# A fused attention and expert kernel on one core: batch 2's loads, the first moves, W0's split and expert 0's first blocks change their places

## The chip, the cores and the metric

The kernel runs on one core of a Trainium2 chip. The metric is the device time of one execution in microseconds (us); less is better. The core has TensorE (PE in the profile; its weight loads are PEld), VectorE (DVE), ScalarE (ACT), GpSimd (POOL) and SyncE (SP). SP computes nothing: it issues nearly all DMA transfers, in the order of the program, and an issue whose data or buffer isn't ready holds every later issue of SP.

## What is computed

Decayed causal attention over 8 batches, 8 heads, 576 positions and a head size of 64, and then a layer of 8 experts with a sticky choice of the expert, on the 8 x 576 tokens of 512 numbers that attention leaves:

```python
decay = cum[:, :, :, None] - cum[:, :, None, :]          # cum: running sum of log(clip(f))
scores = where(causal, -1e9, scale * q @ k.T + decay)
attn = exp(scores - max); attn = attn / (sum + 1e-9)
x = (attn @ v), heads side by side                        # 8 x 576 x 512
# per token: e = argmax of x @ w_gate, or the token before's e if sigmoid(x @ w_local) >= 0.5
p = softmax(x @ w_gate)
out = p[e] * (relu(x @ w1[e]) @ w2[e])                    # w1: 8 x 512 x 1024, w2: 8 x 1024 x 512
```

## The kernel before

**Numbers.** Values that meet on TensorE are split into a float16 high part and a low part (two or three products in place of one). For q, k, v of a batch POOL makes the parts, four to eight instructions each; for weights it is POOL (`early_weights`, four pieces for a block of 128 x 1024) or ACT and DVE (`weights`).

**Attention.** One batch after another. A batch has 25 units (`compute`): the chunks of 128 queries of two heads, and at the end five units for the last 64 queries. A unit runs sc (scores, PE, line L895: a product of `Ak`, `Aq` and one of `KB`, `QB`), mx (DVE L906), ex (ACT L926), tr (PE L941), hi (ACT L946), lo (DVE L950) and av (PE L920). L1001 runs once in a batch, when the last units begin. The order of all instructions of each engine is written out when the program is built: `issue` keeps a clock for each engine and takes the stage that can start first, with weights `W` and ranks `RANK`. So every engine has one fixed list, and an instruction that waits holds all behind it.

**Loads and turns.** q and k of a batch come from memory into `ldq` and `ldk` (L164, L171: 2 transfers of 512 KB and 2 of 64 KB each), POOL splits them into `t16q` and `t16k`, PE turns them (L477, groups of eight tiles: `tq`, `eq`) into `Aq`, `Ak`, and SP copies the high parts into `QB`, `KB` (L397, L394, L401: within SBUF). For batch 0 the turning is done by DMA (L381 to L389). The moves of batch 0 and 1 stand in three hand-written lists, `ORD0`, `ORDA`, `ORDB`; `DUE` gives the times, on the builder's clock, at which the turning of heads 2 and 3, the splits of v and the lists A and B are placed. The move `2` of `ORDB` issues the loads of batch 2, in the middle of batch 0. From then on loads go through the list `bulk`, which `ship` empties, one entry for each unit, when an entry's unit number and condition are met. Copies are kept back (`hold_back`) until the builder's clock has reached the end of what they copy.

**Side work.** `chain` holds the routing of earlier batches (gate products L843, `route`), which `issue` puts between the stages. Routing's `marks` (L1511 to L1525) are DVE's largest. After batch 6's tokens are routed, `early_tok` gathers the first 3 x 128 tokens of experts 0 and 1 (POOL L1677, three buffers) and turns them by DMA (L1679).

**Between attention and experts.** In batch 7 `early_weights` loads (L1642) and splits the first four blocks of expert 0's weights `W0` (all of its w1) on POOL, in portions that `pump` gives out unit by unit; the loads go through three buffers, so that the fourth waits until block 0 is split. Behind attention `flow` orders several streams by their own clocks: `products` (expert 0's and 1's first products, L2087: 8 blocks of 12 matmuls, 128 x 384 each, for either expert), `hidden` (L2122 on ACT, L2124 on DVE), `outputs` (L2102: 3 tiles of 24 matmuls for either expert), the last batch's routing, the rest of the weights (`blocks`, L1851 on ACT and L1855 on DVE) and the gathers of the other tokens (`fetch`, L2178, L2184). The streams have priorities, and PE's list is made of them in the order of the clocks. Then `fixed(0)` (L1709, L1695) and the other experts run, PE nearly without a break.

## Time and profile before

| | |
|---|---|
| time, median of 3 runs | 824.3 us (821.01 to 827.14) |
| the profiled execution's own time | 821.98 us |
| its span, first to last instruction | 820.2 us |
| PE busy | 764.8 us, 93% of the span |
| mean granted clock of TensorE | 0.986 of 2.4 GHz |
| DVE, ACT, POOL busy | 522.6, 437.7 and 398.6 us |
| moved by DMA | 121.99 MB |

All sums are made against 821.98 us. Times of single instructions are us from the start of the span. A timeline row has the start, the duration, the engine, the line, the operation with what it writes and reads, how many, and in brackets the engine's idle time before it and what ended that. PE counts as busy while a matmul is in flight, so a busy PE needn't be at its peak.

### The profile page before, as it was taken

To read this page: it belongs to the slowest core of one execution; us is meant where nothing else is said; L and a number is where in the kernel's file an instruction comes from. 1 tells how busy PE (TensorE), PEld (TensorE's weight loads), DVE (VectorE), ACT (ScalarE), POOL (GpSimd) and SP (SyncE) were. 2 spreads that over 40 slices of the span, in tenths; PEclk is the share of its full clock that TensorE was granted. 3 is DMA by queue.
4 is the path that set the end of the run, shared out by engine and by line. 5 is a ranking of instruction groups with operands and counts; after the bars stand their busy time and mean duration, and the time that the engine had idled before them with its cause. 6 is when DMAs were issued, how large, how long until landed. Compare 5 with 4: busy or idle time off the path is not lost. (4 is left out here: it accounts for less than half of the span.)

```text
span 820.2 us, 21911 instructions
## 1 busy us (share of the span) xinstructions
PE 764.8 (93%) x8918; PEld 544.9 (66%) x8918; DVE 522.6 (64%) x1147; ACT 437.7 (53%) x816; POOL 398.6 (49%) x465
## 2 busy tenths in 40 slices
PE   5798999989999999988879999999999999999996
PEld 3586888877887788866544565675665857667453
DVE  7685879899888999898689813253272744526020
ACT  5595879777887888766633224343241423325121
POOL 9699929388884959572635213131302313031102
PEclk9898999999999999998999999999999999999999
DMA  7969938687594949177693922766282754817101
GB/s 175 192 155 186 216 82 161 156 159 192 106 226 97 186 106 184 26 162 162 122 299 136 266 65 89 187 180 173 101 228 94 192 162 136 218 68 200 53 1 49
DMA packets 195336, 121.99 MB, mean 149 GB/s; under 512 B 135099, under 2 KB 171197, under 8 KB 195212
## 3 DMA queue, kind: packets, MB, share of 16 engines
q1 hardware_dynamic: 189169, 101.42, 54.3%
q0 software_dynamic: 6064, 19.14, 7.2%
q8 instruction: 71, 1.16, 0.6%
q14 instruction: 32, 0.26, 0.1%
HBM read 72.15 MB, written 19.36 MB: 112 GB/s over the span
## 5 line engine op out<-in xcount | busy, mean ns | idle before, releaser
L926 ACT ACTIVATE P<-st,nm 128x512 f32<-128x512 f32 (+3 forms) x288 | 152.9, 587 | 28.4 <-DVE nm L906 25.3
L1696 DVE SCALAR_TENSOR_TENSOR hl<-z,hh 128x608 f16<-128x608 f32 (+5 forms) x64 | 43.0, 673 | 168.1 <-ACT hh L1695 167.2
L1709 PE MATMUL z<-xT,wh 128*128 128x304 f16 (+5 forms) x832 | 147.2, 293 | 1.3 <-DVE hl L1696 1.3
L946 ACT CAST ph<-pt 128x512 f16<-128x512 f32 (+1 forms) x200 | 116.1, 584 | 51.4 <-PE pt L941 46.0
L906 DVE TENSOR_REDUCE nm<-st 128x1 f32<-128x512 f32 (+4 forms) x264 | 134.3, 542 | 14.3 <-PE st L902 11.5
L941 PE MATMUL pt<-ident,P 128*128 128x128 f32 x784 | 122.7, 280 | 7.7 <-DVE pl L950 5.9
L950 DVE TENSOR_TENSOR pl<-pt,ph 128x512 f16<-128x512 f32 x168 | 111.3, 668 | 13.8 <-ACT ph L946 12.2
L1701 POOL DMA_INDIRECT out_dram<-o,ranki x23 | 23.5, 1021 | 168.4 <-ACT o L1700 152.4
L1736 PE MATMUL y<-uh,hl 128*128 128x512 f16 (+2 forms) x440 | 101.0, 309 | 0.3 <-issue 0.3
L941 PEld LDWEIGHTS pt<-ident,P 128*128 128x128 f32 x784 | 84.9, 142 | 24.5 <-issue 6.5
L1736 PE MATMUL y<-uh,hh 128*128 128x512 f16 (+2 forms) x440 | 101.1, 311 | 0.0
L1736 PE MATMUL y<-ul,hh 128*128 128x512 f16 (+2 forms) x440 | 100.8, 309 | 0.0
L1709 PEld LDWEIGHTS <-wh 128*128 128x128 f16 x832 | 81.3, 98 | 29.1 <-issue 1.7
L1709 PE MATMUL z<-xT,wl 128*128 128x304 f16 (+5 forms) x416 | 95.8, 293 | 0.0
L920 PE MATMUL xp<-VH,pl 128*128 128x65 f16 (+1 forms) x960 | 91.5, 195 | 3.5 <-DVE pl L950 3.5
L920 PE MATMUL xp<-VH,ph 128*128 128x65 f16 (+1 forms) x960 | 93.3, 197 | 0.0
L920 PE MATMUL xp<-VL,ph 128*128 128x65 f16 (+1 forms) x960 | 92.2, 196 | 0.0
L1736 PEld LDWEIGHTS <-hh 128*128 128x128 f16 (+2 forms) x880 | 56.7, 100 | 52.7 <-issue 5.2
L920 PEld LDWEIGHTS <-ph 128*128 128x128 f16 (+1 forms) x1920 | 84.6, 103 | 6.8 <-issue 2.8
L1695 ACT ACTIVATE hh<-z 128x608 f16<-128x608 f32 (+5 forms) x64 | 37.3, 583 | 95.5 <-PE z L1709 91.4
L895 PE MATMUL st<-KB,QB 70*128 70x256 f16 (+4 forms) x448 | 78.3, 283 | 8.7 <-DMA KB<-Ak 8.7
L895 PE MATMUL st<-Ak,Aq 128*128 128x256 f16 (+4 forms) x448 | 78.4, 285 | 3.8 <-ACT P L926 2.7
(383 smaller groups left out, 1427.8 us busy)
## 6 DMA issues: line engine op xcount, KB each, us to landing
stg<-in_moe_w_dram SPq DMA_DIRECT2D x64, 512.0 KB
xs<-xr SPq DMA_DIRECT2D x16, 512.0 KB
ldq<-in_q_dram SPq DMA_DIRECT2D x14, 512.0 KB
ldk<-in_k_dram SPq DMA_DIRECT2D x14, 512.0 KB
ldv<-in_v_dram SPq DMA_DIRECT2D x28, 256.0 KB
QB<-Aq SPq DMA_DIRECT2D x15, 256.0 KB
KB<-Ak SPq DMA_DIRECT2D x15, 256.0 KB
ldv<-in_v_dram SPq DMA_DIRECT2D x20, 64.0 KB
```

Of the source, the lines that this page charges most:

```text
L895: nc.tensor.matmul(st[p0:p0 + m, co:co + n], lhsT=queries(lq, kk, h, c), rhs=rhs, start=(ps == 0 and first and co == col), stop=(ps == 1), ...
L906: nc.vector.tensor_reduce(dst, src, axis=AX.X, op=ALU.max, negate=True)
L920: nc.tensor.matmul(xo, lhsT=a[:, c0:c0 + m], rhs=w[:, vi, :], start=False, stop=(i == n - 1 and jj == 2), skip_group_check=True)
L926: nc.scalar.activation(P[:, c0:c1].rearrange("p (k x r) -> p k r x", r=2, x=64), st[:, c0:c1].rearrange("p (k r x) -> p k r x", r=2, x=64) ...
L941: nc.tensor.matmul(U["pt"][:, i * 128:(i + 1) * 128], lhsT=P[:, i * 128:(i + 1) * 128], rhs=ident, is_transpose=True, start=(i == 0), stop ...
L946: nc.scalar.copy(U["ph"][:, :cols], U["pt"][:, :cols])
L950: nc.vector.tensor_tensor(U["pl"][:, :cols], U["pt"][:, :cols], U["ph"][:, :cols], ALU.subtract)
L1695: nc.scalar.activation(hv, z[:, 0:nh, 0:wd], AF.Relu)
L1696: nc.vector.scalar_tensor_tensor(lv, z[:, 0:nh, 0:wd], 0.0, hv, ALU.max, ALU.subtract)
L1701: nc.gpsimd.indirect_dma_start(out=outf, out_offset=bass.IndirectOffsetOnAxis(ap=scat(t), axis=0), in_=o, in_offset=None, bounds_check=NT ...
L1709: nc.tensor.matmul(z[:, a, 0:wd], lhsT=w[:, d, fc * 128:(fc + 1) * 128], rhs=xT[:, x, a * wd:(a + 1) * wd], start=(i == 0), stop=(i == len ...
L1736: nc.tensor.matmul(y[m * r:m * r + m, 0:w], lhsT=a[:, fc, c0:c0 + m], rhs=u[:, fc, w * r:w * r + w], start=(i == 0), stop=(i == len(prods) ...
```

## The change

Batch 2's loads are not issued in `ORDB` any more. The move `2` puts three entries for q and three for k on `bulk`, with the condition that all of batch 1's main groups are turned; what is left of them at the start of batch 1 is issued there, before `prep(2)` adds its own. In `ORD0` the move `sv` (v's heads 6 and 7, POOL) goes to the front, `k:l` (SP) in front of `q:t4`, `q:p` (POOL) behind `sp`, and `q:M` (SP) in front of `k:t`; `ORDA` and `ORDB` swap three pairs. Three times of `DUE` change. `PB` makes POOL's portions of W0 end at unit 14 in place of 23. `z_lines` puts the first `NZ` = 3 of expert 0's 8 product blocks into batch 7's list from unit 12 on: four stages of three matmuls, one ACT and one DVE stage for each block, in a bank of `psS`, not before `early_tok` plus 10.5 us on the builder's clock and not before POOL's queue is given out; `products` and `hidden` begin with block 3. In `flow` PE's routing steps are planned as if what they wait for came 1.5 us later (`LATE`). `SX` and `SQ` leave the value 0 that was there. Core of the diff:

```diff
--- before.py
+++ after.py
@@ -40,9 +40,9 @@
 
 
 
-ORD0 = moves_of("q:l :k2 q:t4 k:l q:p k:t4 :sp q0:m :sv k:p q:c k:c q1:m q:t k:t :lm q:M k:m :at 0:R 1:R :lv")
-ORDA = moves_of("q0:P k:M 0:V 1:V k:ag")
-ORDB = moves_of("q:ag q:G0 2:V q1:P k0:P k1:P q:e k:e 3:V q:G1 k:G0 :vl :Vl q:2 k:G1 :iv v0:P k:2")
+ORD0 = moves_of("q:l :k2 :sv k:l q:t4 k:t4 :sp q:p q0:m k:p q:c k:c q1:m q:t q:M k:t :lm k:m :at 0:R 1:R :lv")
+ORDA = moves_of("k:M q0:P 0:V 1:V k:ag")
+ORDB = moves_of("q:ag q:G0 2:V q1:P k0:P k1:P k:e q:e 3:V q:G1 k:G0 :vl :Vl k:G1 q:2 :iv v0:P k:2")
 
 GM, GW = 8, 500
 
@@ -60,12 +60,19 @@
 HB = (1, 1)
 ST = 4
 XP = 20
+PB = 14
+NZ = 3
+LATE = 1500
+SX = {}
+SQ = [0]
+Z0 = 12
+ZT = 10500
 XG = 6
 NP0 = 4
 SB = 3
 
 T0 = 9700.0
-DUE = (("k2", 11000), ("q2", 12500), ("k3", 14500), ("q3", 15500), ("v", 18000), ("v4", 20500), ("a", 26000), ("b", 29000))
+DUE = (("k2", 11000), ("q2", 12500), ("k3", 14500), ("q3", 15000), ("v", 18000), ("v4", 19500), ("a", 26000), ("b", 30000))
 
 NB = (4, 5, 4)
 NOV = 31
@@ -664,10 +671,17 @@
         elif a == "sv":
             split_v(6, 8)
         elif a == "2":
-            new_load(2, b)
-            for C in range(2):
-                load_main(2, b, C, 0, H)
-            load_last(2, b)
+            c = lambda: all((1, x, j) in turned for x in 'qk' for j in range(4))
+
+            def some(C):
+                if C == 0:
+                    new_load(2, b)
+                if C < 2:
+                    load_main(2, b, C, 0, H)
+                else:
+                    load_last(2, b)
+
+            bulk.extend([(0, c, lambda C=C: some(C)) for C in range(3)])
         elif a == "R":
             same_rows(int(b))
         elif a == "t4":
@@ -1152,7 +1166,7 @@
 
     WAIT = {("PE", "PE"): 0, ("PE", "ACT"): 197, ("PE", "DVE"): 196, ("ACT", "PE"): 227, ("ACT", "ACT"): 150,
             ("ACT", "DVE"): 141, ("DVE", "PE"): 200, ("DVE", "ACT"): 128, ("DVE", "DVE"): 127}
-    STAGES = ("sc", "mx", "mn", "ex", "tr", "hi", "lo", "sub", "lo2", "av", "n1", "n2", "tq", "eq")
+    STAGES = ("sc", "mx", "mn", "ex", "tr", "hi", "lo", "sub", "lo2", "av", "n1", "n2", "tq", "eq", "z0", "z1", "z2", "z3", "zh", "zl")
     RANK = {st: 0.0 for st in STAGES + ("side",)}
     RANK["side"] = -20
     RANK.update({'sc': 24.3, 'mx': 16.8, 'mn': -67.5, 'ex': 93.3, 'tr': -65.0, 'hi': 26.5, 'lo': -10.3, 'sub': 17.2, 'lo2': 31.3, 'av': 16.7, 'n1': 33.1,
@@ -1160,6 +1174,8 @@
     W = {st: 0 for st in RANK}
     W.update({'sc': -210, 'mx': -60, 'mn': -710, 'ex': -30, 'tr': -180, 'hi': -210, 'lo': -140, 'sub': -410, 'lo2': -360, 'av': -130, 'n1': -200,
               'n2': -170, 'tq': -210, 'eq': -50})
+    RANK.update({'z0': 90, 'z1': 90, 'z2': 90, 'z3': 90, 'zh': 90, 'zl': 90})
+    W.update({'z0': 300, 'z1': 300, 'z2': 300, 'z3': 300, 'zh': 0, 'zl': 0})
     clock = {"PE": T0, "ACT": T0, "DVE": T0, "POOL": T0}
     due = deque()
     pools = {}
@@ -1176,7 +1192,11 @@
         after = []
         if st == "tq":
             after.append((u["ready"], "POOL"))
-        elif prev is not None or st != "sc":
+        elif st == "z0":
+            if queue or "ready" not in EX:
+                return None
+            after += [(EX["ready"], "POOL"), (clock["POOL"], "POOL")]
+        elif prev is not None or st not in ("sc", "z0"):
             dep = (n, prev) if prev is not None else (n - 1, "ex")
             if dep not in ends:
                 return None
@@ -1226,7 +1246,7 @@
 
         if t is None:
             return 0
-        return SW[0] if cost is POOL or t <= clock[eng] + SW[2] else SW[1]
+        return SW[0] if cost is POOL or t <= clock[eng] + SQ[0] else SW[1]
 
     def side_issue(t, eng, cost):
         fn = chain[0]
@@ -1777,13 +1797,57 @@
         EX["p"] = probs(invp[:, :, 0:NE], NE, "x")
 
     def early_tok():
+        EX["ready"] = max(clock["DVE"], clock["POOL"]) + ZT
         for e in range(2):
             xT = EX["xT", e] = ep.tile([128, 8, 128 * EARLY], F16, name=f"xT{e}")
             tokens(ep, xT, lambda i: EX["g"][:, CAP * e + i:CAP * e + i + 1], EARLY, (B - 2) * S)
 
+    HID = {}
+    EM = 128 * EARLY
+
+    def z_part(fc, z, i0, i1):
+        wh, wl = W0[0:2]
+        prods = [(w, d, x) for d in range(ND) for w, x in ((wh, d), (wh, ND + d), (wl, d))]
+        for i in range(i0, i1):
+            w, d, x = prods[i]
+            nc.tensor.matmul(z, lhsT=w[:, d, fc * 128:(fc + 1) * 128], rhs=EX["xT", 0][:, x], start=(i == 0), stop=(i == len(prods) - 1))
+
+    def z_unit(fc):
+        Z = {}
+
+        def mm(k):
+            if k == 0:
+                Z["z"] = psS.tile([128, 512], F32, name="st")[:, 0:EM]
+            z_part(fc, Z["z"], 3 * k, 3 * k + 3)
+
+        def hh():
+            if fc == 0:
+                HID["hh", 0] = ep.tile([128, NF, EM], F16, name="hh")
+                HID["hl", 0] = ep.tile([128, NF, EM], F16, name="hl")
+            nc.scalar.activation(HID["hh", 0][:, fc], Z["z"], AF.Relu)
+
+        def hl():
+            nc.vector.scalar_tensor_tensor(HID["hl", 0][:, fc], Z["z"], 0.0, HID["hh", 0][:, fc], ALU.max, ALU.subtract)
+
+        u = {f"z{k}": ("PE", 490, lambda k=k: mm(k), {"psS": 1} if k == 0 else {}, {}) for k in range(4)}
+        u["zh"] = "ACT", 400, hh, {}, {}
+        u["zl"] = "DVE", 480, hl, {}, {"psS": 1}
+        return u
+
+    def z_lines():
+        for fc in range(NZ):
+            n, prev, u = serial[0] + 100 + fc, None, z_unit(fc)
+            for st in ("z0", "z1", "z2", "z3", "zh", "zl"):
+                line[st].append((n, u, prev))
+                prev = st
+
     gated = set()
     for b in range(B):
+        SQ[0] = SX.get(b, 0)
         units = compute(b, Tq[b])
+        if b == 1:
+            while bulk and bulk[0][0] == 0:
+                bulk.popleft()[2]()
         if 0 < b < B - 1:
             queue.extend(prep(b + 1))
         for i, u in enumerate(units):
@@ -1793,9 +1857,11 @@
                 init_gate()
             if not due:
                 if b < B - 1 or i < XP:
-                    pump((23 if b == B - 1 else 25) - i)
+                    pump((PB if b == B - 1 else 25) - i)
                 ship(i if i < 24 else 99)
                 add_turns(i)
+            if b == B - 1 and i == Z0:
+                z_lines()
             step(u)
             if b == B - 1:
                 if i == 5:
@@ -2039,7 +2105,7 @@
                     after.append(h[3])
                 if op.get("opens"):
                     after.append(lock["free"])
-                t = max([clk.get(eng, t0), op.get("from", 0) + t0] + [e + (0 if src == eng else 200 if src != "SP" else 0) for e, src in after])
+                t = max([clk.get(eng, t0), op.get("from", 0) + t0] + [e + (LATE if eng == "PE" and op.get("seq", True) and h[0] < -4999 else 0) + (0 if src == eng else 200 if src != "SP" else 0) for e, src in after])
                 able.append((t, h[0], h))
             first = min(able, key=lambda x: x[0])
             t, _, h = min((x for x in able if x[2][2]["eng"] == first[2][2]["eng"] and x[0] <= first[0] + 300), key=lambda x: x[1])
@@ -2065,8 +2131,6 @@
         return dict(eng=eng, cost=cost, fn=fn, needs=needs, gives=gives, **kw)
 
     XP0 = EX["xT", 0], EX["xT", 1]
-    HID = {}
-
     def products():
 
         m = 128 * EARLY
@@ -2074,8 +2138,7 @@
             W = W0 if e == 0 else EX["W"]
             wh, wl, uh, ul = W
             xT = XP0[e]
-            hh = hl = None
-            for fc in range(NF):
+            for fc in range(NZ if e == 0 else 0, NF):
                 n = NF * e + fc
                 prods = [(w, d, x) for d in range(ND) for w, x in ((wh, d), (wh, ND + d), (wl, d))]
                 for c in range(0, len(prods), 2):
@@ -2087,7 +2150,7 @@
                             nc.tensor.matmul(HID["z", n][:, 0, 0:m], lhsT=w[:, d, fc * 128:(fc + 1) * 128], rhs=xT[:, x, 0:m],
                                              start=(i == 0), stop=(i == len(prods) - 1))
                     needs = [("hl", n - 2)] if c == 0 and n > 1 else []
-                    if fc == 0:
+                    if fc == (NZ if e == 0 else 0):
                         needs += [("w", e, prods[c + 1][1])]
                     yield op_("PE", 330, fn, needs, [("z", n)] if c + 2 == len(prods) else [])
             for t in range(EARLY):
@@ -2112,11 +2175,11 @@
     def hidden(part):
 
         m = 128 * EARLY
-        for n in range(2 * NF):
+        for n in range(NZ, 2 * NF):
             def fn(n=n):
                 e, fc = divmod(n, NF)
                 if part == 0:
-                    if fc == 0:
+                    if ("hh", e) not in HID:
                         HID["hh", e] = ep.tile([128, NF, m], F16, name="hh")
                         HID["hl", e] = ep.tile([128, NF, m], F16, name="hl")
                     nc.scalar.activation(HID["hh", e][:, fc], HID["z", n][:, 0, 0:m], AF.Relu)
@@ -2258,7 +2321,7 @@
         yield from blocks(first, NP, ST + 3 - NP, 1)
 
     FW = static_weights(W0, 0, NP0, ahead=SB, ha=HB)
-    ready = op_(None, 0, nop, gives=[("w", 0, d) for d in range(ND)])
+    ready = op_(None, 0, nop, gives=[("w", 0, d) for d in range(ND)] + [("hl", n) for n in range(NZ)])
     e0 = CAP + EARLY
     flow([(-9000, iter([ready])), (-3000, products()), (-6000, hidden(0)), (-6000, hidden(1)), (-4400, outputs(0)), (-4400, outputs(1)),
           (-5600, routing()), (-5000, third_pair()), (-5500, blocks(FW, NP0, SB, 0)), (-300, second()), (-4400, second_rest()),
```

## Rows read from the trace of the kernel before

**Rows 1.** Page, part 1: busy time, share of the span, instructions

```profile
PE 764.8 (93%) x8918; PEld 544.9 (66%) x8918; DVE 522.6 (64%) x1147; ACT 437.7 (53%) x816; POOL 398.6 (49%) x465
```

**Rows 2.** PE's waits, whole span: us in total, times, longest

```profile
PE st L895 <- DMA KB<-Ak: 8.7, 3, 5.0
...
PE psG L1582 <- ACT kg L1420: 2.3, 1, 2.3
PE psG L1445 <- DVE crow L1441: 2.0, 1, 2.0
```

**Rows 3.** Windows, two early stops: length, busy us (instructions), PEclk, DMA share, GB/s

```profile
30.50:36.00 5.50, 0.50 (x8) 0.27 (x5) 1.65 (x3) 1.42 (x4) 1.28 (x4) 0.95 1.13 241
...
70.50:74.00 3.50, 0.10 (x1) 0.20 (x2) 0.65 (x2) 0.19 (x1) 3.40 (x4) 0.85 1.19 171
74.00:80.00 6.00, 6.00 (x76) 4.50 (x76) 2.90 (x6) 2.44 (x5) 5.39 (x8) 0.52 0.87 142
```

**Rows 4.** SP's timeline, batch 2's first load and batch 1's copy

```profile
56.19 1.21 SPq L164 DMA_DIRECT2D ldq<-in_q_dram  x2
...
66.77 2.78 SPq L394 DMA_DIRECT2D KB<-Ak  x2
```

**Rows 5.** PE's timeline, batch 1's first scores

```profile
73.90 0.59 PE L895 MATMUL st<-KB,QB 70*128 70x512 f16 x1 [3.40 <-DMA KB<-Ak]
```

**Rows 6.** Line L1001, batches 0, 1, 2: min/median/max ns, first to last start

```profile
L1001 PE MATMUL st<-mB,mA x4: 193/193/203, 55.7 to 55.8; 128*128 128x64 f16 x4
...
L1001 PE MATMUL st<-mB,mA x4: 193/193/203, 106.5 to 106.6; 128*128 128x64 f16 x4
...
L1001 PE MATMUL st<-mB,mA x4: 193/193/202, 149.8 to 149.9; 128*128 128x64 f16 x4
```

**Rows 7.** Windows of batch 1 and its end; columns as in rows 3

```profile
80.00:100.00 20.00, 19.85 (x297) 17.02 (x295) 18.18 (x42) 17.42 (x36) 19.20 (x23) 1.00 1.00 192
...
105.00:120.00 15.00, 14.75 (x308) 12.36 (x307) 12.14 (x30) 11.86 (x26) 3.33 (x3) 1.00 0.21 44
```

**Rows 8.** Windows, attention's last 15 us and the transition

```profile
393.00:408.00 15.00, 11.79 (x257) 9.28 (x257) 10.09 (x24) 10.10 (x21) 11.42 (x10) 1.00 0.60 111
408.00:440.00 32.00, 25.11 (x199) 13.80 (x193) 26.48 (x70) 10.05 (x18) 15.95 (x15) 1.00 0.87 266
```

**Rows 9.** POOL's timeline in batch 7: first gather, block 3's split

```profile
382.18 1.24 POOL L1677 DMA_INDIRECT xg<-xs,xg  x1 [10.36 <-DVE xs L1617]
...
408.42 1.04 POOL L1651 TENSOR_SCALAR stg<-stg 128x1024 f32<-128x1024 f32 x1
```

**Rows 10.** DVE's timeline, the same operation with POOL busy and idle

```profile
367.62 1.50 DVE L1525 TENSOR_TENSOR LO<-i,lo 128x640 f16<-128x640 f16 x1
...
441.31 1.55 DVE L1525 TENSOR_TENSOR LO<-i,lo 128x640 f16<-128x640 f16 x2
```

**Rows 11.** Windows of L2087 alone: length, PE and PEld busy, PEclk, DMA

```profile
415.00:420.00 5.00, 4.77 (x30) 2.64 (x27) 1.00 0.95 234
450.00:460.00 10.00, 8.79 (x55) 5.40 (x56) 1.00 0.88 164
```

**Rows 12.** DVE's timeline, last splits of expert 0's w2, expert 1's w1

```profile
431.44 1.20 DVE L1855 SCALAR_TENSOR_TENSOR ul<-stg,uh 128x1024 f16<-128x1024 f32 x1
...
445.08 1.22 DVE L1855 SCALAR_TENSOR_TENSOR wl<-stg,wh 128x1024 f16<-128x1024 f32 x1
```

**Rows 13.** SP's and ACT's timelines, expert 0's other tokens and their first use

```profile
449.52 7.03 SPq L2184 DMA_TRANSPOSE xT<-xg  x2
...
484.48 0.38 ACT L1695 ACTIVATE hh<-z 128x256 f16<-128x256 f32 x1 [0.57 <-PE z L1709]
```

**Rows 14.** SP's and PE's timelines, batch 6's turn, fourth load, gate products

```profile
367.82 1.86 SPq L778 DMA_TRANSPOSE xt<-xr  x1
...
371.65 2.13 SPq L1642 DMA_DIRECT2D stg<-in_moe_w_dram  x1
...
377.26 0.90 PE L843 MATMUL st<-wg,xt 128*128 128x18 f16 x30
```

## The prediction

> **What bounds the kernel now.** I read the page's busy times first: PE has 764.8 us of 820.2 [rows 1], so the time is PE's work plus the places where PE stands still or runs at the lower of its two clock levels. The chain that ended last shows only the last 20 us, where the output drains, and the change touches nothing there. So I took PE's waits over the whole span and asked which of them the edits reach. Three belong to them: 8.7 us of scores behind a DMA copy into `KB`, in three waits, and 2.3 and 2.0 us of routing steps in the transition [rows 2].
>
> The windows then price the two long `KB` waits. In 30.5 to 36 (batch 0's fifth head) PE is busy for 0.50 of 5.50 us, in 70.5 to 74 (batch 1's first scores) for 0.10 of 3.50, and in the six us after the second the mean granted clock is 0.52, so PE does at 1.2 GHz what it does at 2.4 elsewhere [rows 3]. Why the second copy is late stands in SP's list: the loads of batch 2 begin at 56.19, the copy into `KB` is issued at 66.77 [rows 4], and DMA works at a share above 1 while PE waits [rows 3]. The product that needed the copy starts at 73.90, 7.1 us after the issue [rows 4, 5]. The third `KB` wait is what is left of 8.7 after 5.0 and 3.4, 0.3 us [rows 2, 5]: that is batch 2's start, where DMA's share in the 15 us around it is 0.21 [rows 7].
>
> At the other end I read the windows of attention's last 15 us and of the transition: PE idles 15 - 11.79 = 3.2 us and 32 - 25.11 = 6.9 us [rows 8].
>
> **The change, part by part.**
>
> *Batch 2's loads behind batch 1's copies.* It takes 8 transfers, 4 x 512 and 4 x 64 KB or 2.36 MB, out of the way of the copies. What it gives back is the idle 3.4 us [rows 5] and half of what the lower clock cost: six us at 0.52 hold 6 x 0.52 = 3.1 us of full-speed work, so 2.9 lost [rows 3]. Together 6.3. A second price comes from L1001, which runs once a batch: 55.7, 106.5 and 149.8, so 50.8 us for the step that holds the wait and 43.3 for the next [rows 6]; 7.5 apart. I take 6.5, less what the copies still wait where nothing is ahead of them, 0.3, already within the rounding. The lower bound is 2, if the copies still meet loads that the builder's clock lets go too soon (the condition looks at the turning, not at the copies); the upper is 7.5.
>
> *The same loads, later.* POOL needs q of batch 2 in batch 1. It is busy 19.20 of 20 us in 80 to 100, but only 3.33 of 15 in 105 to 120 [rows 7], so some 11 us of lateness have cover there, and 2.36 MB at the 192 GB/s of 80 to 100 take 12.3 us at the outside, at the 241 of rows 3 9.8. PE isn't held by POOL's lateness at once: what POOL makes there is for batch 2. DMA is the tighter cover: share 1.00 in 80 to 100, then 15 x (1 - 0.21) = 11.9 us idle [rows 7], of which a batch 2 that starts 6.5 us sooner leaves 5.4. So batch 2's own copies can be late by nothing (the loads move at a better rate while they are alone) or by up to 12.3 - 5.4 = 6.9. I take 0.5, near the lower end, because a share of 1.13 to 1.19 in rows 3 shows that 1.00 isn't all that DMA can carry.
>
> *The first moves and `DUE`.* In front of the copy that PE waits for in 30.5 to 36 stand the same transfers as before, in another order; on POOL the same instructions are permuted; the due times shift by 0.5 to 1 us. The two issues of `k:l` go ahead of a turn and cost a turn what two issues take, 1.2 us in the nearest row [rows 4]. Bounds: 1.2 lost, or the same 1.2 gained because k's turn no longer stands behind `k:l`. I take 0; PE's idle 5 us there stay.
>
> *W0 split sooner.* In the trace POOL stands idle for 10.36 us before the first gather at 382.18, and block 3 is split only from 408.42 [rows 9], when attention is over. With `PB` 14 all 16 pieces go out by unit 13, so blocks 2 and 3 fall into that idle time (four pieces at 1.04 us and more each, about 5 us a block), and the gathers stay where they are, or at most a piece or two later. No time by itself; it is what lets the product blocks start before 408. The nearest row on what POOL does to DVE: a mark of routing took 1.50 us beside POOL's pieces and two took 1.55 later, with POOL idle [rows 10], so 0.7 us each. In 372 to 382 DVE reads scores from PSUM; I take nothing for it, with 0.7 us to either side. The Trainium skill (SBUF — State Buffer, section "SBUF: two separate sides") says that DVE and GpSimd share one pair of ports under an exclusive lock and that the loser waits for the whole instruction; by it, marks that came to lie beside blocks 2 and 3 would lose that 0.7 us each, up to 2 us, and it speaks against this edit. The trace agrees as far as the two rows go, but marks already lie beside blocks 0 and 1.
>
> *Three product blocks in batch 7's list.* 36 matmuls at 4.77 us for 30 [rows 11], 0.16 each, are 5.7 us of PE work that leave the transition. They meet 3.2 us of idle PE in attention's last 15 us [rows 8]; what doesn't fit, 2.5 us, makes attention end later, so 3.2 is gained if the transition stays as dense as it is. `LATE` aims at the 2.3 and 2.0 us of routing waits [rows 2], another 4.3 at best. But the transition can't shrink by all of 7.5: expert 1's products begin about 451.2 (8.79 of the ten us to 460) [rows 11], and the last split of its w1 ends at 446.3 [rows 12], paced by DMA and DVE and not by PE: 4.9 at most. Before it, expert 0's last w2 split ends at 432.6 [rows 12], which holds its first output tile when the products are done sooner. I take 4.0, between 0 and 4.9. The routing itself gets slower by up to 1.5 us at each of about nine PE steps, 13.5; its tokens are issued for turning by 456.6 and first used shortly before 484.5 [rows 13], so that cover holds.
>
> *Sum.* -6.5 + 0.5 + 0 - 4.0 = -10.0: 821.98 - 10.0 = 812.0. The execution's own time lies 2.3 us under the median of 824.3; against that median the same gain would give 814.3.
>
> **The rivals.**
>
> *B. The transition pays nothing.* It is bound by weights and DVE (26.48 busy of 32 us, rows 8), the product blocks only lengthen attention's tail. For it: DMA's share of 0.87 there [rows 8]. Against it: the 4.9 us between split and use [rows 11, 12]. Time: 821.98 - 6.5 + 0.5 = 816.
>
> *C. The wait moves to batch 2.* The loads that left 57 to 70 end up ahead of batch 2's copies; with the full 6.9 us and half of about 6 us at the lower clock, 3, batch 1's gain is gone: 821.98 - 6.5 + 9.9 - 4.0 = 821.4; with half of the wait, 3.5, and the clock kept, 815.0. For it: DMA's share of 1.00 through batch 1. Against it: 11.9 idle us before batch 2's copies [rows 7]. The Trainium skill (DMA: Bandwidth & Descriptors, section "Queues, rings and completion order") says that each DMA engine consumes a queue's descriptors in ring order, so SP's copies can't pass SP's loads; the 7.1 us of batch 1's copy agree, and by the rule alone C would be the likelier the fuller the queue is.
>
> *D. Slower: the fourth weight load holds SP.* It needs block 0's buffer back from POOL and stands at 371.65, behind batch 6's second turn at 367.82 [rows 14]. With faster portions it is written out about three units sooner; ahead of the turn it would hold it until after 371.65 + 2.13, 6 us later. The gate products read the turned tokens at 377.26, 9.4 us after the turn's issue [rows 14]. It decides once the turn is later than the part of these 9.4 us that the transfer leaves free. Priced in full: PE waits 6, loses 3 to the clock, gathers come 6 later, and the product blocks, whose places in PE's list are fixed, wait 6 and lose 3 again: 18, and no gain there: 821.98 - 6.0 + 18 = 834. Against it: the turn stands in the same queue ahead of the pieces.
>
> **How the numbers follow.** Forecast 0.56 (807 to 816), B 0.15, C 0.17, D 0.07; 0.05 for less than 807, where the wait of 30.5 to 36 shrinks too. The range that leaves out 2 in 10 is 805 to 821.5; the forecast's own is 807 to 816. About 1% is what a measurement of this kernel can tell from no change; 1% of 821.98 is 8.2, so faster means below 813.8. Three quarters of the forecast, the 0.05 and a part of B, whose batch 1 may give 7.5, lie there: 0.54. Slower is D and an accident of the new order elsewhere, 0.08. Same is the rest, 0.38.
>
> **What would show it.** In the profile after: the loads L164 of batch 2 behind L394 in SP's list, no `KB` wait at batch 1 and no lower clock after it, some 43 to 45 us between the first two L1001. At batch 2's start a `KB` wait under 1 us; several would be C. Blocks 2 and 3 split before the first gather, 36 matmuls 128 x 384 before attention's end, expert 1's products within 5 us after the last split of its w1. If these start no sooner than 451 less what batch 1 gave, B holds; a wait of L843 behind a turn is D. If 30.5 to 36 looks the same, the first moves are worth nothing.

## The result and the profile after

| | before | after |
|---|---|---|
| median of 5 runs | 823.24 us (821.01 to 827.14) | 815.48 us (815.01 to 816.57) |
| the profiled execution's own time | 821.98 us | 815.01 us |
| its span | 820.2 us | 813.2 us |

The ratio after to before is 0.9904, with a 95% interval of 0.9874 to 0.9933; in a later set of runs on another chip it was 0.9938 (0.9915 to 0.9961). Forecast were 10.0 us less than the profiled execution of before; measured are 7.0 less. PE runs as many instructions; its busy time is 2.4 us less, its idle time 4.6 less (55.4 to 50.8 us of the span).

The page's busy times after, against [rows 1], and three of PE's waits over the whole span (us in total, times, longest), against [rows 2]:

```profile
PE 762.4 (94%) x8918; PEld 543.1 (67%) x8918; DVE 526.1 (65%) x1147; ACT 438.3 (54%) x816; POOL 398.2 (49%) x465
```

```profile
PE st L909 <- DMA KB<-Ak: 6.4, 2, 4.0
...
PE z L2150 <- DVE hl L1830: 1.2, 1, 1.2
...
PE y L2165 <- DVE crow L1455: 0.6, 1, 0.6
```

The wait for the copy into `KB` (L895 is now L909) went from 8.7 us in three to 6.4 in two. One of the two is the old one in batch 0. Batch 1's 3.4 us are gone. The other stands at batch 2's first scores, where before only 0.3 us were waited. The routing waits of 2.3 and 2.0 us are down to 0.6.

The line that runs once a batch, L1001, is now L1015. Its first three batches after, against [rows 6]:

```profile
L1015 PE MATMUL st<-mB,mA x4: 193/194/203, 54.1 to 54.2; 128*128 128x64 f16 x4
...
L1015 PE MATMUL st<-mB,mA x4: 193/194/204, 98.7 to 98.8; 128*128 128x64 f16 x4
...
L1015 PE MATMUL st<-mB,mA x4: 194/194/203, 145.6 to 145.7; 128*128 128x64 f16 x4
```

The steps were 50.8 and 43.3 us; they are 44.6 and 46.9. Batch 1 gave 6.2, batch 2 took 3.6 back. The next four steps are the same to 0.1 us, the last one 0.6 longer (53.9 to 54.5). From the last start of this line to the first product of `fixed(0)` it was 483.0 - 390.5 = 92.5 us and is 475.3 - 386.9 = 88.4; from there to the end of the span 337.2 and 337.9. With the 1.6 us by which the first start is earlier this makes the 7.0: 1.6 + 6.2 - 3.6 - 0.6 + 4.1 - 0.7.

SP's timeline after, batch 1's copy and the first of batch 2's loads, then a batch later batch 3's k and the copy for batch 2:

```profile
64.65 3.27 SPq L401 DMA_DIRECT2D KB<-Ak  x2
...
68.62 1.34 SPq L171 DMA_DIRECT2D ldq<-in_q_dram  x2
...
103.27 1.30 SPq L171 DMA_DIRECT2D ldk<-in_k_dram  x2
104.61 2.72 SPq L178 DMA_DIRECT2D ldk<-in_k_dram  x2
...
110.95 0.94 SPq L401 DMA_DIRECT2D KB<-Ak  x1
```

The loads stand behind batch 1's copies, as meant. But 35 us later four loads of batch 3's k stand ahead of batch 2's copies. PE's timeline and the windows (length, busy time of PE, PEld, DVE, ACT, POOL, granted clock, DMA share, GB/s) show what that does, against [rows 3, 5]:

```profile
116.32 0.38 PE L909 MATMUL st<-KB,QB 70*128 70x512 f16 x1 [2.38 <-DMA KB<-Ak]
```

```profile
30.50:36.00 5.50, 1.49 (x20) 0.99 (x19) 2.31 (x4) 1.67 (x4) 1.46 (x5) 0.92 1.11 259
...
68.00:80.00 12.00, 12.00 (x216) 9.90 (x209) 10.89 (x23) 9.38 (x21) 7.86 (x8) 1.00 1.02 243
...
105.00:113.50 8.50, 8.16 (x212) 7.22 (x208) 6.07 (x15) 6.98 (x14) 7.36 (x34) 1.00 1.00 227
113.50:120.00 6.50, 4.12 (x35) 2.89 (x29) 3.20 (x8) 2.21 (x6) 6.17 (x7) 0.78 1.14 191
```

In 68 to 80 PE has no idle time and the full clock. In 113.5 to 120 it has 2.38 us of idle time, and a granted clock of 0.78 costs 6.5 x 0.22 = 1.4 more: 3.8, about the 3.6 by which the step grew. The copy took 116.32 - 110.95 = 5.4 us from issue to use, with DMA at a share of 1.00 and above around it.

In the transition: the three product blocks in the list are L1813. The line over the whole span, and the same from 404.55 us on, where attention's last product is done:

```profile
L1813 PE MATMUL st<-xT,wh x24: 325/327/337, 398.0 to 409.6; 128*128 128x384 f16 x24
L1813 PE MATMUL st<-xT,wl x12: 325/326/327, 398.4 to 409.8; 128*128 128x384 f16 x12
...
L1813 PE MATMUL st<-xT,wh x22: 326/327/337, 404.6 to 409.6; 128*128 128x384 f16 x22
L1813 PE MATMUL st<-xT,wl x11: 325/327/327, 404.9 to 409.8; 128*128 128x384 f16 x11
```

Only 3 of the 36 matmuls lie inside attention; 33 run directly behind it.

### The profile page after: what moved, and what is told of

Its sections match the earlier page's. It is cut to its first block, busy times and chain, and to the rows that moved or that the text cites. A ratio compares the mean times of both kernels' runs of the same rounds, so it can differ in the third digit from the quotient of the medians.

```text
span 813.2 us, 21913 instructions
## 1 busy us (share of the span) xinstructions
PE 762.4 (94%) x8918; PEld 543.1 (67%) x8918; DVE 526.1 (65%) x1147; ACT 438.3 (54%) x816; POOL 398.2 (49%) x465
## 5 line engine op out<-in xcount | busy, mean ns | idle before, releaser
L1756 PEld LDWEIGHTS <-hh 128*128 128x128 f16 (+2 forms) x880 | 56.8, 100 | 53.3 <-issue 5.8
L909 PE MATMUL st<-KB,QB 70*128 70x256 f16 (+4 forms) x448 | 77.7, 281 | 6.4 <-DMA KB<-Ak 6.4
L909 PE MATMUL st<-Ak,Aq 128*128 128x256 f16 (+4 forms) x448 | 77.9, 284 | 3.6 <-ACT P L940 2.5
```

Of the source, the lines that this page charges most:

```text
L909: nc.tensor.matmul(st[p0:p0 + m, co:co + n], lhsT=queries(lq, kk, h, c), rhs=rhs, start=(ps == 0 and first and co == col), stop=(ps == 1), ...
L1756: nc.tensor.matmul(y[m * r:m * r + m, 0:w], lhsT=a[:, fc, c0:c0 + m], rhs=u[:, fc, w * r:w * r + w], start=(i == 0), stop=(i == len(prods) ...
```

## The experiments

Each kernel ran beside the kernel before, and those of one set on one chip: e1, e2, e5, e6; e3, e4, e8, e7; after_again, e10, e9; e11. "Step 1" and "step 2" are those of the once-a-batch line in the profiled execution, "start" its first start, "wait" PE's wait for `KB<-Ak` in total.

| kernel | median us (n) | ratio to before, 95% | start | step 1 | step 2 | wait |
|---|---|---|---|---|---|---|
| before | 823.24 (5) | | 55.7 | 50.8 | 43.3 | 8.7 |
| after | 815.48 (5) | 0.9904 (0.9874-0.9933) | 54.1 | 44.6 | 46.9 | 6.4 |
| e1_loads_only | 816.53 (6) | 0.9945 (0.9922-0.9967) | 53.3 | 44.6 | 47.4 | 6.4 |
| e2_loads_back | 816.67 (7) | 0.9957 (0.9939-0.9976) | 54.8 | 52.6 | 43.3 | 10.3 |
| e6_order_only | 820.26 (10) | 1.0004 (0.9990-1.0019) | 53.7 | 51.0 | 43.2 | 8.5 |
| e5_k3_behind | 810.36 (4) | 0.9894 (0.9856-0.9932) | 53.6 | 44.5 | 43.7 | 3.6 |
| e7_first_load_behind | 813.46 (4) | 0.9883 (0.9841-0.9926) | 54.2 | 46.5 | 43.9 | 0.4 |
| e9_last_keys_early | 810.41 (4) | 0.9889 (0.9863-0.9915) | 52.2 | 44.5 | 43.4 | 3.9 |
| after_again | 814.47 (6) | 0.9938 (0.9915-0.9961) | 55.2 | 44.5 | 46.4 | 7.0 |

**The loads alone, and all but the loads.** e1 puts this into the kernel before, e2 takes it out of the kernel after:

```diff
-            new_load(2, b)
-            for C in range(2):
-                load_main(2, b, C, 0, H)
-            load_last(2, b)
+            c = lambda: all((1, x, j) in turned for x in 'qk' for j in range(4))
...
+            bulk.extend([(0, c, lambda C=C: some(C)) for C in range(3)])
...
```

> The kernel before with only batch 2's loads put behind batch 1's copies; first moves, W0 and transition as before. Theory L (the loads' place alone makes both the gain of batch 1 and the loss of batch 2): the step between the first two starts of the line that runs once a batch falls from 50.8 to 44.5-45.5 us, the next one grows from 43.3 to 46-47.5, the third stays at 53; time 823.2 - 6 + 3.3 = 820.5. Rival O (the new order of the moves carries part of it): the first step is 47 or longer, time 822.5 or more.

> The changed kernel with batch 2's loads issued where they were, everything else changed. Theory L: first step 50-51 us, second 43-43.5, a wait of 3 us or more for the copy into KB at batch 1 and none over 0.5 at batch 2; time 815.5 + 2.6 = 818. Rival O (with the new order the copies of batch 1 come out ahead of the loads or late for another reason): the first step stays under 48, time 815.5 or less.

Both came out as theory L, but for e2's step 1, which is 1.6 us over its range: the place of the loads alone moves step 1 and step 2, whatever the order of the moves. The medians lie 3.8 and 3.7 us under that of the kernel before in the same set (820.35), so the loads and the rest share the gain about equally; 0.9945 x 0.9957 = 0.990, the ratio of the whole change in its first set (in the later one it was 0.9938). In time e1 gave 3.8 where 2.7 were expected; the steps of its trace account for 94.1 - 92.0 = 2.1 of it, and its start came sooner. e2 came out at 816.67 where 818 were expected.

PE's timeline and a window of e2 show batch 1's wait back with its low clock:

```profile
74.64 0.59 PE L902 MATMUL st<-KB,QB 70*128 70x512 f16 x1 [5.11 <-DMA KB<-Ak]
```

```profile
70.00:80.00 10.00, 5.36 (x73) 4.43 (x74) 3.08 (x7) 2.45 (x5) 7.33 (x7) 0.53 0.96 162
```

**The order of the first moves alone.** The kernel before with the three lists and `DUE` of the kernel after.

> The kernel before with only the three hand-written lists and the due times changed. Theory M (the order shortens the start by itself): the first start of the once-a-batch line falls from 55.7 to 54.1, the wait before 35.9 from 5.0 to 4.0, the steps stay 50.8 and 43.3; time 823.2 - 1.6 = 821.6. Rival N (the start is shorter only because batch 2's loads are gone from batch 0): 55.7 within 0.3, time 823.2.

In the profile it looks like theory M: the first start came at 53.7. The times say no change, 1.0004 with an interval of 0.0015 to either side. The table settles it: with the old lists the first start was 55.7 in one execution and 53.3 in another (e1), with the new ones anywhere from 53.4 (e3) to 56.2 (e8). The 1.6 us between the two first traces lie inside this spread, and no gain of the order is shown.

**Batch 3's k behind batch 2's copies.** The trick of the change carried on for one batch more:

```diff
+                late = b == 2 and nm == "k"
+                ok = (lambda: all((2, x, j) in turned for x in "qk" for j in range(5))) if late else (lambda nm=nm: nm in done)
+                i = 0 if late else i
...
```

> The changed kernel with batch 3's k loads put behind batch 2's copies, as the change did with batch 2's loads and batch 1's copies. Theory K (the copy into KB at batch 2 is late because k's loads of batch 3, issued at 103 to 105 us, go ahead of it): the copy lands within 3.5 us of its issue, the wait of 2.4 us at batch 2 is under 0.5, the granted clock of 113 to 120 is over 0.9, the second step is 43.5-44.5 us in place of 46.9; time 815.5 - 3 = 812.5, if the later k loads hold POOL in batch 2 by nothing. Rival P (the copy is late because POOL was late, waiting 4.0 us for q's loads and 3.1 for the gate weights, so that everything of batch 2 is turned later): the wait stays over 1.5 us and the step over 46; time 815.5. Third case: the lateness moves on to batch 3, whose step grows by 2 or more; time 815 to 816.

SP's and PE's timelines of this kernel, and the window that stood at 4.12 us of PE and a clock of 0.78:

```profile
110.67 0.48 SPq L401 DMA_DIRECT2D KB<-Ak  x1
```

```profile
113.80 0.38 PE L912 MATMUL st<-KB,QB 70*128 70x512 f16 x1
```

```profile
113.50:120.00 6.50, 6.17 (x62) 4.90 (x61) 6.21 (x15) 4.94 (x11) 6.20 (x8) 1.00 0.93 206
```

Theory K holds, and P falls on the issue: the copy is issued at 110.67 as against 110.95 and is in use 3.1 us later as against 5.4. The semaphore updates in the traces tell when a transfer landed: in the kernel after the four loads landed at 108.6 to 112.4 us, then the copies into `QB`, then this one at 116.3, in the order of issue; in e5 it landed at 113.8. POOL was as late in e5 (it waited 3.58 us for q's loads and 3.26 for the gate's weights). So batch 2's copies were not late because POOL was; they stood behind four loads. Step 3 is 53.3 as against 52.9, so at most 0.4 us moved on to batch 3.

**One load more, in batch 0.** e7 adds to e5 that `q0:m`, the first half of batch 1's q, goes behind the second copies into `QB` and `KB` (a part of the line `ORD0`):

```diff
-q:p q0:m k:p q:c k:c q1:m
+q:p k:p q:c k:c q0:m q1:m
```

> The kernel with batch 3's k behind batch 2's copies, and one load more moved: the first 512 KB of batch 1's q, issued at 27.3 us ahead of batch 0's second copies into QB and KB, goes behind them. Theory K carried on (a copy behind loads on SP is late by what they move; 512 KB at 200 GB/s are 2.6 us): PE's wait at 31.5 us falls from 3.6 to 1-1.5 us, the first start of the once-a-batch line comes 2.5-3.5 us sooner; batch 1 keeps 0 to 2 of that back because POOL gets q later; time 810.4 - 2 = 808.4. Rival G (the copy isn't held by the load but by the turn ahead of it, issued at 24.3, or by the 900 to 1000 us^-1 small packets of the copy itself): the wait stays 3 us or more and POOL gets q 3 us later; time 810.4 to 812.

Half of theory K: the wait of 3.6 us was gone (the 0.4 left is at batch 2's start), and the time wasn't, with a ratio of 0.9883 as against e5's 0.9894. PE's timeline and the windows show the place:

```profile
53.86 0.42 PE L912 MATMUL st<-KB,QB 70*64 70x64 f16 x8 [3.90 <-DMA QB<-augt]
```

```profile
48.00:52.00 4.00, 1.96 (x41) 1.71 (x37) 2.04 (x4) 3.72 (x7) 3.92 (x4) 0.98 0.89 138
52.00:56.00 4.00, 2.14 (x18) 1.21 (x19) 0.78 (x2) 0.00 (x0) 3.54 (x11) 0.50 0.52 117
56.00:60.00 4.00, 4.00 (x37) 2.46 (x36) 2.28 (x7) 2.06 (x5) 3.92 (x4) 0.67 0.38 76
```

The last 64 keys and queries of batch 0 come by four small transfers that SP issues at 48.9 to 52.1 us, behind batch 1's v. PE came sooner and waited there instead, and the clock after that wait (0.50 and 0.67) made step 1 two us longer. A wait taken away was a wait moved, as in batch 2.

**Those four transfers sooner.** e9 is e7 with `k:e q:e` moved from `ORDB` to `ORD0`, behind `at`.

> The kernel with the first load of batch 1's q behind batch 0's copies, and now also batch 0's last copies (the last 64 keys and queries and their decay rows, four transfers, read at 53.9 us after a wait of 3.9) issued some 11 us sooner, right behind the decay table. Theory K2 (the 3.6 us won at 31.5 were lost again only there, with the lower clock after it, 0.50 and 0.67 in 52 to 60): no wait of 1 us or more between 32 and 60, first start of the once-a-batch line 49.5-51, the next step 44.5-45.5; time 813.5 - 5 = 808.5. Rival H (POOL's splits of batch 1's k end at 52 us whatever PE does, so PE waits for batch 1's turned heads or copies next): first start 50-51 but the next step 48 or more; time 811 to 813.

One of PE's waits over the whole span, the windows that answer to e7's, and the first start:

```profile
PE st L912 <- DMA KB<-Ak: 3.9, 2, 3.5
```

```profile
52.00:56.00 4.00, 4.00 (x61) 2.55 (x56) 3.82 (x11) 3.87 (x10) 3.19 (x3) 1.00 0.87 178
56.00:60.00 4.00, 4.00 (x62) 3.34 (x59) 3.58 (x9) 3.25 (x8) 3.69 (x7) 1.00 0.64 122
```

```profile
L1018 PE MATMUL st<-mB,mA x4: 193/193/203, 52.2 to 52.2; 128*128 128x64 f16 x4
```

The wait at 50 to 54 and its low clock are gone, and the first start is the earliest of all, 52.2; rival H falls, step 1 is 44.5. The four transfers went out at 40.9 to 45.8 us, 6 to 8 sooner and not 11, since the decay rows wait for the table. K2 is right in kind, not in size: a wait of 3.5 us stands at 31 us again, though the load is behind the copy as in e7. Its length depends on when PE comes as well as on the copy: PE came to this product, the first scores of batch 0's fifth head, at 30.2 us in e9 and at 31.5 in e5. In e7, where the clock was lower on the way (0.83 in 24 to 30, 1.00 in e9), it came at 32.95 and found the copy done. PE's timelines of e7 and of e9:

```profile
32.95 0.38 PE L912 MATMUL st<-KB,QB 70*128 70x512 f16 x1
```

```profile
33.70 0.38 PE L912 MATMUL st<-KB,QB 70*128 70x512 f16 x1 [3.50 <-DMA KB<-Ak]
```

In the twelve traces with the load ahead of the copy this product starts at 34.95 to 36.68 us, so the load's place does bring it sooner, by 1.2 us or more. What spreads the start among those twelve stays open. All four runs of e9 (808.32 to 810.94) lie under all six of the changed kernel beside it (812.52 to 816.30): 4.1 us between the medians, and the best kernel of this study together with e5. That e9 beats e5 isn't shown; the two ratios are 0.9889 and 0.9894.

**The transition's three edits.** One constant each: `PB` 14 or 23 (W0 split sooner), `NZ` 3 or 0 (blocks in the list), `LATE` 1500 or 0.

> The changed kernel without the three product blocks in batch 7's list (all eight are planned behind attention); the early split of W0 and the 1.5 us of LATE stay. In the trace after, only 3 of the 36 matmuls lie inside attention, 33 run from 404.6 us on, behind it. Theory S (the sooner split pays, since the blocks can run as soon as attention ends, wherever they are listed): from the last start of the once-a-batch line to the first product of the fixed experts stays 88.4 us within 1; time 815.5 to 816.5. Rival Z (the place in the list pays, as the forecast had it): that stretch grows by 3 to 4 us to 91.5-92.5; time 819.

> The changed kernel with LATE 0, the three blocks and the early split staying. Theory W (LATE moves PE's routing steps behind products and so takes their waits away): waits of PE for kg and crow of 2 us each come back, the stretch from the last start of the once-a-batch line to the fixed experts grows from 88.4 to 91-92.5 us; time 818.5. Rival V (expert 1's last weight split at 444.6 us ends the stretch, so waits ahead of it cost nothing): it stays within 1 us; time 815.5.

> The changed kernel with neither the three blocks in the list nor LATE: of the transition's edits only the sooner split of W0 stays. Theory S: most of the 4.1 us is in the split, so the stretch from the last start of the once-a-batch line to the fixed experts is 89-90 us; time 817. Rival: it needs the other two, the stretch is 91-92.5 as in the kernel before; time 819.

> The changed kernel once more, beside the other two on one chip. Both theories of the transition use it as the level: ratio to the kernel before 0.990 with 0.003 either way; in its trace 88 to 88.8 us from the last start of the once-a-batch line to the fixed experts if 88.4 is typical, over 89.5 if one trace says little about this stretch.

> The changed kernel with LATE 0 once more, beside the changed kernel itself. Theory W (LATE carries most of the transition's gain, as the medians of the earlier runs say): 2.5 to 4.5 us more than the changed kernel, ratio 0.994-0.996; in the trace the stretch to the fixed experts is 91 us or more and a wait for kg or crow of 1.5 us or more stands in it. Theory V2 (the blocks in the list and LATE pay 1.5 to 2 us each, as the single traces say): 1.5 us more, ratio 0.992, stretch 89.5-90.2.

> The changed kernel with LATE alone of the transition's edits: W0's portions go out until unit 23 as before, no blocks in batch 7's list. Theory W (LATE carries the transition's gain): ratio 0.990-0.992, as without the blocks alone (0.9898), and the stretch from the last start of the once-a-batch line to the fixed experts 88-89.5 us, with no wait for kg or crow over 1 us. Rival U (LATE needs products that are ready early to fill PE while routing is put off, and with W0's last block split only behind attention they aren't): ratio 0.994 or more, stretch 90.5-92.5, a wait for a split of W0 in it.

The stretch in the profiled execution to the first product of `fixed(0)`, from the last start of the once-a-batch line, and from the one before it, which leaves POOL's portions in batch 7 no part in the choice of the mark:

| kernel | sooner | blocks | `LATE` | from the last | from the one before | median us, ratio |
|---|---|---|---|---|---|---|
| before, e1, e6 | no | no | no | 92.5, 91.0, 91.4 | 146.4, 144.5, 145.2 | |
| e8 | yes | no | no | 92.1 | 146.6 | 819.60, 0.9957 |
| e11 | no | no | yes | 89.3 | 144.6 | 816.85, 0.9949 |
| e3 | yes | no | yes | 90.6 | 145.0 | 815.05, 0.9898 |
| e4, e10 | yes | yes | no | 89.9, 92.8 | 144.5, 146.7 | 818.61, 816.22; 0.9948, 0.9955 |
| after, after_again | yes | yes | yes | 88.4, 88.1 | 142.9, 142.1 | 815.48, 814.47; 0.9904, 0.9938 |

Where all three edits stand, in e2, e5, e7 and e9 too, the stretch from the last start is 88.0 to 88.4 us in six traces of six. With none, or one or two of them, it is 89.3 to 92.8. Their waits say why. Of e8, between 403 and 450 us:

```profile
PE psG L1465 <- DVE crow L1461: 2.0, 1, 2.0
PE psG L1602 <- ACT kg L1440: 1.9, 1, 1.9
```

Of e4, without `LATE`, in the same stretch, and of e3, without the blocks:

```profile
PE psG L1465 <- DVE crow L1461: 1.7, 1, 1.7
PE psG L1480 <- DVE so L1475: 1.4, 1, 1.4
...
PE y L2165 <- DVE cin L1470: 1.1, 1, 1.1
```

```profile
PE z L2150 <- DVE hl L2187: 3.0, 1, 3.0
```

Without `LATE` PE waits for steps of the routing. With `LATE` but without the blocks those waits are gone, and PE, which now does products in their place, comes too soon to a product whose bank DVE hasn't emptied: 3.0 us in e3, 3.8 in two waits in e11. With the blocks in the list, the first three are through when `flow` begins, and 1.2 and 0.5 us of such waits are left. The sooner split alone is worth nothing (92.1 and 146.6, as before). In a kernel that has the sooner split and the blocks, `LATE` is worth 1.8 to 3.6 us by the times beside the changed kernel's (816.22 against 814.47 in one set; 0.9948 against 0.9904 across two). Without them it shows no gain in time: e11's 0.9949 is no less than the ratio of the loads alone (e1, 0.9945), as rival U had it, though the wait for a split that U named isn't in e11's trace, and its stretch of 89.3 fits W. With `LATE` and the sooner split, e3 lies 4.5 us under e8, which has the split alone, in one set: the two pay together. What the blocks are worth stays open: the trace of e3 says 2.2 us, its times say nothing (0.9898), and its profiled execution was the longest of its four (816.45; the others down to 813.62). One trace can't tell 2.2 us here: e4 and e10 are the same program, and their stretches are 89.9 and 92.8.

## Why the prediction came out as it did

The forecast of 812.0 was 3.0 us under the profiled execution. The range held it; the size is nearer to rival C with half of the wait (815.0) than to the forecast, and the mechanism of C is what the traces show. A part of the 7.0 us is luck: 1.6 of them are the earlier first start, for which e6's times show no gain, and the medians of the later set lie 820.29 - 814.47 = 5.8 us apart.

- **Batch 1, -6.5: right**, 6.2. The copy's wait and the low clock after it went together, as the windows priced them, and e1 and e2 move them alone. The end of the copy's lateness is also seen directly: with the loads behind, 68 to 80 us has none in the trace of after.
- **The same loads, later, +0.5: the step that failed**, 3.6: the wait grew from 0.3 to 2.4, and the clock cost 1.4. The bounds 0 to 6.9 held it; the choice near the lower end did not. Its reason, that a share of 1.13 to 1.19 leaves room above 1.00, misreads the column: a share is the time that packets took, not what was moved, and 1.19 went with 171 GB/s [rows 3], 1.00 with 192 [rows 7]. The cover was counted as DMA's idle time in 105 to 120, the whole stretch around batch 2's start [rows 7]. But the idle time that counts is the one ahead of the copies. In the kernel after none was left there (a share of 1.00 in 105 to 113.5), and what filled it wasn't batch 2's loads but the next ones in the chain: batch 3's k is let go when POOL is done with batch 2's k, POOL stood idle 3.97 us for batch 2's q and 3.10 for the gate's weights behind it in the queue, and so these loads came out just ahead of the copies. Every queue entry whose condition hangs on the moved one had to be moved along in the sum. The rule that the Trainium skill gives (DMA: Bandwidth & Descriptors, section "Queues, rings and completion order"), that each DMA engine consumes a queue's descriptors in ring order, made C likelier the fuller the queue is, and the traces agree: 5.4 us from issue to use behind four loads, 3.1 without them (e5).
- **The first moves, 0: right.** e6 measures 1.0004.
- **The split sooner, no time by itself: right**, e8. Blocks 2 and 3 went into POOL's idle time, the first gather came at 377.17 in place of 382.18 [rows 9], with 0.34 us of idle time ahead of it in place of 10.36:

```profile
377.17 1.24 POOL L1697 DMA_INDIRECT xg<-xs,xg  x1 [0.34 <-DVE xs L1637]
```

  The 0.7 us that POOL's pieces might cost a step of DVE did come, but not to the marks of [rows 10]: these lie beside block 1 in both kernels and take 1.50 and 1.30 us, before and after. Two short routing steps came to lie beside block 3 and took 0.79 and 1.02 us in place of 0.14 and 0.17, when POOL was idle [rows 9]. The second one in DVE's timeline before and after, and the last two pieces of block 3 in POOL's after:

```profile
381.70 0.17 DVE L1615 TENSOR_SCALAR xg<-xt 128x9 int32<-128x9 f32 x1
```

```profile
375.85 1.02 DVE L1635 TENSOR_SCALAR xg<-xt 128x9 int32<-128x9 f32 x1
```

```profile
374.57 2.27 POOL L340 TENSOR_TENSOR wl<-stg,wh 128x512 f16<-128x512 f32 x2
```

  The step ends at 376.87, as the last piece does (376.84). It delayed little, since the gather at 377.17 stands behind that piece on POOL anyway.
- **Blocks and `LATE`, -4.0: right in sum (4.1, of which batch 7 gave 0.6 back), wrong in one reason.** Attention's idle 3.2 us [rows 8] were hardly filled: 2.3 are left in the 15 us up to 404.55, and 33 of 36 matmuls run after it. What went is the transition's own idle time: 6.9 of 32 us [rows 8], 2.9 after:

```profile
403.40:435.40 32.00, 29.07 (x263) 16.35 (x258) 23.70 (x57) 10.80 (x20) 13.18 (x12) 1.00 0.88 263
```

  The waits for routing [rows 2] went, as `LATE` aims at, and the blocks may pay by sparing `flow` its first waits for `hl`, which is argued from e3's and e11's waits and not shown by their times. Rival B falls with e2: all but the loads gives 3.7 us, and the order of the moves none of it (e6). The bound that expert 1's last split of w1 sets was reached: DVE starts it at 443.42, expert 1's products are running by then, and PE waits 0.2 us for it, where before some 5 us lay between [rows 11, 12]. DVE's and PE's timelines after:

```profile
443.42 1.22 DVE L1921 SCALAR_TENSOR_TENSOR wl<-stg,wh 128x1024 f16<-128x1024 f32 x1
```

```profile
444.69 0.34 PE L2150 MATMUL z<-xT,wl 128*128 128x384 f16 x1 [0.21 <-DVE wl L1921]
```

- **Rival D: its order came and cost nothing.** The fourth weight load stands ahead of the turn, as D feared. SP's timeline after:

```profile
361.73 0.33 SPq L1662 DMA_DIRECT2D stg<-in_moe_w_dram  x1
362.12 3.37 SPq L792 DMA_TRANSPOSE xt<-xr  x1
```

POOL's timeline says why, block 0's first and last pieces:

```profile
356.85 1.04 POOL L1671 TENSOR_SCALAR stg<-stg 128x1024 f32<-128x1024 f32 x1 [0.80 <-PE pt L955]
...
359.10 2.60 POOL L340 TENSOR_TENSOR wl<-stg,wh 128x512 f16<-128x512 f32 x2
```

Block 0's buffer was free at 359.10 + 2.60 = 361.70, and the load was issued at once. SP had waited 1.8 us for it, the turn went out right behind, and PE shows no wait for the turned tokens. D let the load wait until its old time, 371.65; but the portions that bring the issue forward bring the release forward too.

## What to carry over

Moving loads out of the way of one copy can put other loads in the way of the next: follow each entry that is let go by it to the next place where something short is waited for, and count only the idle time of the queue ahead of that place. When the cost of such a wait is read, the half clock behind it belongs to it. Before a gain in a single trace is believed, look at how far the same mark moves between executions in which nothing changed there.

## What the runs showed of the hardware

Two things weren't expected. The wait in batch 0 at 31 us differs from execution to execution: in the seven traces whose kernels give the same instructions up to there (after, after_again, e3, e4, e8, e10, e11) it was 2.5 to 5.3 us, and the first start of the once-a-batch line 53.4 to 56.2. And one short wait costs more than its length: in e7 the granted clock was 0.50, the lower level of 1.2 GHz, already in the last 1.9 us of the wait of 3.9, and then 0.61 on average from 53.86, where the wait ended, to 60. That is 6.14 x 0.39 = 2.4 us of full-speed time behind a wait of 3.9.
